# VectorE computes one head's exps in 53 of 512 attention bursts

## Chip, cores, metric

The kernel runs on one core of one Trainium2 chip. The metric is the device time of one execution in microseconds (us). Executions of one kernel agree here within about 0.3%. A trace is one profiled execution; its span is 1.7 to 1.8 us shorter than the time of the same execution. Engines: PE is TensorE (PEld its weight loads), ACT is ScalarE, DVE is VectorE.

## The reference

The result mixes a state-space layer and an attention layer by a gate, `g * a + (1 - g) * b`, over 2048 rows of 1024 columns. What matters here is the attention `b`: 32 heads of 32 columns, no mask.

```python
q, k, v = qkv[0], qkv[1], qkv[2]
scores = jnp.einsum("bhqd,bhkd->bhqk", q, k) * (Dh ** -0.5)
p = _softmax(scores, axis=-1)
o = jnp.einsum("bhqk,bhkd->bhqd", p, v)
```

The exps of 32 x 2048 x 2048 scores are most of ScalarE's work. The layer `a`, the projections and the output product are "dense" work that TensorE does between the attention's parts.

## The kernel before

The attention is cut into 512 bursts of four heads, 256 keys and 256 queries. A burst has three parts: eight score matmuls, two exps of 128x1024 (two heads each), and value sums in four quarters of four matmuls. Scores live in three PSUM slots of two banks. A burst takes two slots, so the scores of the next burst must wait until the first exp of this one has freed its slot.

```python
def burst(self, B):
    sl = [(2 * self.p) % 3, (2 * self.p + 1) % 3]
    # ... eight score matmuls into slots sl[0] and sl[1] ...
    for z in range(2):
        s, p = sl[z], self.pt_of(B, z)
        self.act(lambda e, s=s, p=p: e.activation(self.tile[p], ps[:, 2 * s:2 * s + 2, :],
                 ACT.Exp, scale=SCALE), [("S", s)], [("pt", p)], "exp")
```

Bank 6 holds the value sums. Bank 7 is the only bank of the dense work. A dense "chain" is eight matmuls of 512 columns (or sixteen, with four small diagonal ones) that accumulate in bank 7; VectorE then evicts it, and the next chain's first matmul must wait for that eviction. Each burst of the main loop is ordered so:

```python
for p in range(first, NBURST):
    self.burst(p)                       # scores, then the two exps
    q0, q1 = self.quarters[p]
    self.pv(q0, q1)                     # value sums of burst p-2, in general 4 quarters
    if q1 % 32 == 0:
        self.normalize(q1 // 32 - 1)    # VectorE
    # ... DMA issues ...
    while used < quota:                 # quota 4: four dense matmuls, in order
        # ... choose a chain where none is open ...
        wt, f = cur.pieces.pop(0)
        f()
        used += wt
        # ...
    # ... VectorE's background work, as much as fits the period ...
    if ended is not None:
        ended.evac()                    # VectorE evicts bank 7
```

## Time and profile before

| | before |
|---|---|
| time, median | 961.46 us |
| ACT busy | 944.0 of 960.1 us |
| start of one burst's first exp to the next burst's, from burst 128 on | 1.833 us |
| so one 128x1024 exp occupies ACT's pipe for | 0.917 us |
| length of that exp's record in steady state | 1.326 us |

The last two rows need care. Exp records overlap: one is 1.326 us long, yet the next starts 0.917 us later. A record therefore holds some queueing behind its predecessor.

Next, the timeline of the kernel before over one burst in which a new dense chain begins (start us, length us, engine, line, operation; in brackets the idle time before and what ended it). L1393 evicts bank 7, L1559 is the scores, L1582 the value sums, L1386 the dense matmuls.

```profile
465.86 0.69 DVE L1393 CAST f_Q<-f_ps 128x512 bf16<-128x512 f32 x1 [2.94 <-PE f_ps L1386]
465.89 0.12 PEld L1559 LDWEIGHTS f_ps<-f_Q,f_K 32*128 32x128 bf16 x8 [0.56 <-ACT f_pt L1565]
466.22 0.47 PEld L1582 LDWEIGHTS f_ps<-f_V,f_pt 128*128 128x128 bf16 x16 [0.21 <-issue]
466.61 0.55 PEld L1386 LDWEIGHTS f_ps<-f_xT,f_wb 128*128 128x128 bf16 x4
...
467.72 0.12 PEld L1559 LDWEIGHTS f_ps<-f_Q,f_K 32*128 32x128 bf16 x8 [0.56 <-ACT f_pt L1565]
```

The reader should see two things. The scores are released by ACT, so TensorE has slack at the end of the burst. And the eviction starts slightly before the scores and ends at 466.55.

### The profile page before, as it was taken

To read this page: it belongs to the slowest core of one execution; us is meant where nothing else is said; L and a number is where in the kernel's file an instruction comes from. 1 tells how busy PE (TensorE), PEld (TensorE's weight loads), DVE (VectorE), ACT (ScalarE), POOL (GpSimd) and SP (SyncE) were. 2 spreads that over 40 slices of the span, in tenths; PEclk is the share of its full clock that TensorE was granted. 3 is DMA by queue.
4 is the path that set the end of the run, shared out by engine and by line. 5 is a ranking of instruction groups with operands and counts; after the bars stand their busy time and mean duration, and the time that the engine had idled before them with its cause. 6 is when DMAs were issued, how large, how long until landed. Compare 5 with 4: busy or idle time off the path is not lost.

```text
span 960.1 us, 33364 instructions
## 1 busy us (share of the span) xinstructions
PE 928.0 (97%) x15316; PEld 490.1 (51%) x15316; DVE 513.2 (53%) x1097; ACT 944.0 (98%) x1034; POOL 10.1 (1%) x39
## 2 busy tenths in 40 slices
PE   8899999999999999999999999999999999999996
PEld 4555644564444554555545654544645556444443
DVE  2788888898888427112188711178836112232223
ACT  6999999999999999999999999999999999999996
POOL 2000000000000000000000000000000000000000
PEclk9999999999999999999999999999999999999998
DMA  9558434210133002220023210133101213123312
GB/s 203 96 103 131 77 59 85 60 28 29 49 67 79 17 8 62 58 53 17 18 52 62 59 40 24 43 85 60 40 6 39 84 38 118 51 80 118 106 59 72
DMA packets 157074, 60.88 MB, mean 63 GB/s; under 512 B 145664, under 2 KB 145664, under 8 KB 156928
## 3 DMA queue, kind: packets, MB, share of 16 engines
q1 hardware_dynamic: 154768, 58.16, 27.0%
q8 instruction: 121, 1.98, 0.9%
q10 hardware_dynamic: 2160, 0.53, 0.3%
q14 instruction: 25, 0.20, 0.1%
HBM read 16.79 MB, written 12.58 MB: 31 GB/s over the span
## 4 chain that ended last, share of the span: by engine, by line
ACT 96%; SPq 1%; PE 1%; DVE 1%; DMA 1%; issue 0%; DVEq 0%
ACT f_pt L1565 89%; ACT f_OT L1565 2%; ACT f_Et L1565 2%; ACT f_cT_re L1565 2%; ACT f_cT_im L1565 2%; SPq L1040 1%; DMA f_xT<-in_A_x_dram 1%; PE f_ps L1559 0%; PE f_ps L1789 0%; PE f_ps L1582 0%; PE f_ps L1161 0%; PE f_ps L1416 0%; DVE f_xT L1828 0%; PE f_ps L1121 0%; PE f_ps L1815 0%
## 5 line engine op out<-in xcount | busy, mean ns | idle before, releaser
L1565 ACT ACTIVATE f_pt<-f_ps 128x1024 bf16<-128x1024 f32 x944 | 867.1, 1309 | 0.6 <-PE f_ps L1559 0.6
L1582 PEld LDWEIGHTS f_ps<-f_V,f_pt 128*128 128x128 bf16 x7552 | 220.2, 96 | 99.2 <-issue 98.8
L1582 PE MATMUL f_ps<-f_V,f_pt 128*128 128x33 bf16 x7552 | 268.7, 178 | 0.0
L1559 PE MATMUL f_ps<-f_Q,f_K 32*128 32x256 bf16 x4096 | 203.3, 273 | 22.7 <-ACT f_pt L1565 4.4
L1559 PEld LDWEIGHTS f_ps<-f_Q,f_K 32*128 32x128 bf16 x4096 | 60.5, 92 | 224.2 <-ACT f_pt L1565 205.8
L1416 PE MATMUL f_ps<-f_xT,f_wb 128*128 128x512 bf16 x512 | 131.0, 377 | 0.5 <-DVE f_pf L1211 0.4
L1386 PE MATMUL f_ps<-f_xT,f_wb 128*128 128x512 bf16 x464 | 118.9, 378 | 0.0
L1335 DVE TENSOR_TENSOR_SCAN f_ht<-f_pf,f_init,f_ut 128x512 bf16<-128x512 f32 x64 | 80.8, 1273 | 0.0
L1458 DVE TENSOR_SCALAR f_Ag<-f_ps,f_gcol 128x512 f32<-128x512 f32 x32 | 24.0, 751 | 91.0 <-PE f_ps L1445 91.0
L1445 PE MATMUL f_ps<-f_cT_im,f_hp 128*128 128x512 bf16 x192 | 72.6, 378 | 0.0
L1445 PE MATMUL f_ps<-f_cT_re,f_hp 128*128 128x512 bf16 x192 | 72.6, 378 | 0.0
L1595 DVE RECIPROCAL f_rc<-f_ps 128x8 f32<-128x8 f32 x63 | 13.1, 208 | 107.3 <-PE f_ps L1582 107.1
L1476 PE MATMUL f_ps<-f_wb,f_OT 128*128 128x512 bf16 x252 | 65.8, 380 | 0.0
L1404 PE MATMUL f_ps<-f_wb,f_xT 128*128 128x128 bf16 x896 | 59.2, 219 | 0.0
L1416 PEld LDWEIGHTS f_ps<-f_xT,f_wb 128*128 128x128 bf16 x512 | 40.5, 96 | 31.9 <-issue 0.4
L1482 DVE SCALAR_TENSOR_TENSOR f_xT<-f_ps,f_gcol,f_hp 128x512 bf16<-128x512 f32 (+1 forms) x28 | 21.0, 750 | 62.5 <-PE f_ps L1476 62.5
L1422 DVE CAST f_ub<-f_ps 128x512 bf16<-128x512 f32 x48 | 33.2, 691 | 39.7 <-PE f_ps L1416 39.7
L1386 PEld LDWEIGHTS f_ps<-f_xT,f_wb 128*128 128x128 bf16 x464 | 36.3, 96 | 27.9
L1404 PEld LDWEIGHTS f_ps<-f_wb,f_xT 128*128 128x128 bf16 x896 | 50.4, 97 | 0.0
L1326 DVE TENSOR_TENSOR f_tq<-f_ht,f_Et 128x512 bf16<-128x512 bf16 x128 | 45.8, 416 | 0.0
L1393 DVE CAST f_Q<-f_ps 128x512 bf16<-128x512 f32 x30 | 20.7, 692 | 46.7 <-PE f_ps L1386 46.5
L1326 DVE TENSOR_TENSOR f_ut<-f_tq 128x512 f32<-128x512 bf16 x64 | 42.2, 683 | 0.0
(130 smaller groups left out, 619.8 us busy)
## 6 DMA issues: line engine op xcount, KB each, us to landing
ag_scratch<-f_Ag SPq DMA_DIRECT2D x32, 256.0 KB, 2.3
f_hp<-ag_scratch SPq DMA_DIRECT2D x32, 256.0 KB, 2.8
f_wb<-in_B_wqkv_dram SPq DMA_DIRECT2D x21, 256.0 KB, 4.2
out_dram<-f_xT SPq DMA_DIRECT2D x16, 256.0 KB, 2.1
f_wb<-in_B_wo_dram SPq DMA_DIRECT2D x1, 1024.0 KB, 5.5
f_OT<-f_On SPq DMA_TRANSPOSE x63, 2.3
f_wb<-in_B_wo_dram SPq DMA_DIRECT2D x1, 768.0 KB
f_wb<-in_B_wqkv_dram ACTq DMA_DIRECT2D x2, 256.0 KB, 4.0
```

The source lines that it names most:

```text
L1326: ops.append((c, lambda: dve(lambda e: e.tensor_tensor(o, a, b, op), r, w)))
L1335: ops.append((1.29, lambda ri=ri: dve(lambda e: e.tensor_tensor_scan(ht[:, ri, :], rr, ut[:, ri, :], self.init[:, ri, j:j + 1], ALU.mult, ...
L1386: mms.append((1, lambda e, f, l, a=a: e.matmul(ps[:, bank, :], w[:, g % 2, part, a, :], xT[:, a, 512 * ch:512 * (ch + 1)], start=f, stop=l ...
L1404: m = e.matmul(ps[:, bank, 128 * q:128 * (q + 1)], xT[:, a, 128 * kt:128 * (kt + 1)], w[:, g % 2, 2, a, :], start=(a == 0), stop=(a == 7))
L1416: mms.append((1, lambda e, f, l, a=a: e.matmul(ps[:, 7, :], bT[:, n % 2, ri, a, :], xT[:, a, 512 * ch:512 * (ch + 1)], start=f, stop=l), [ ...
L1422: self.dve(lambda e: e.tensor_copy(self.ub[k][:, ri, :], ps[:, 7, :]), [("bank", 7)], [("ub", k, ri)] + over, "evac_u")
L1445: mms.append((1, lambda e, f, l, j=j, ri=ri: e.matmul(ps[:, 7, :], hp[:, ri, j, cols], cT[ri][:, j, 512 * cb:512 * (cb + 1)], start=f, sto ...
L1458: self.dve(lambda e: e.tensor_scalar(a, ps[:, 7, :], self.gcol[:, 0, tt:tt + 1], None, ALU.mult), [("bank", 7), "g0"], [at], "evac_c")
L1476: mms.append((1, lambda e, f, l, j=j: e.matmul(ps[:, 7, :], OT[:, j, 256 * qb + 128 * r:256 * qb + 128 * (r + 1)], wo[j][0][:, 512 * cb:51 ...
L1559: m = e.matmul(ps[:, 2 * sl[h // 2] + h % 2, 256 * kl:256 * (kl + 1)], K[32 * h:32 * h + 32, g % 2, 128 * kt:128 * (kt + 1)], Q[32 * h:32 ...
L1565: self.act(lambda e, s=s, p=p: e.activation(self.tile[p], ps[:, 2 * s:2 * s + 2, :], ACT.Exp, scale=SCALE), [("S", s)], [("pt", p)], "exp")
L1582: m = e.matmul(ps[:, 6, o:o + 33], self.tile[p][:, h2, 256 * kl + 128 * qt:256 * kl + 128 * (qt + 1)], V[:, g % 2, 2 * i + kl, h, :], star ...
```

## The change

The intent is to relieve ScalarE. In 53 bursts (one in four, in stretches where VectorE has little else: bursts 173 to 185, 205 to 253, 297 to 329, 401 to 505) ScalarE computes only one of the first tile's two heads. VectorE computes the other: the scaled score goes to a 32-bit integer, its upper half gives the exponent bits, its lower half feeds a cubic. TensorE's work is moved to make the changed burst short (planned at 1.41 us instead of 1.83): it gets three dense matmuls and three value quarters, the burst before it five and three, and later bursts five quarters. Value sums may now lag, so a tile's last value sums are ordered ahead of the exp that refills it.

```diff
+DPERIOD = 1.41
+for lo, hi, m in ((172, 188, 4), (204, 254, 4), (296, 332, 4), (400, 508, 4)):
+    out += [B for B in range(lo, hi) if B % m == 1]          # DVB, 53 bursts
 ...
+def dve_exp(self, B, s, p):
+    # over: at the first use of each of three tile sets, the former users of that space
+    self.act(lambda e: e.activation(t[:, 0, :], ps[:, 2 * s, :], ACT.Exp, scale=SCALE), [("S", s)], [("pt", p)] + over, "exp")
+    self.dve(lambda e: e.tensor_scalar(xi, ps[:, 2 * s + 1, :], EXP_A, EXP_B, ALU.mult, ALU.add), [("S", s)], [("xi", k)] + over, "exp_a")
+    self.dx += [  # put into VectorE's order later, where they fit
+        (0.48, ... e.tensor_scalar(hi, hi, 0.0, 128.0, ALU.max, ALU.mult) ...),        # exp_b
+        (0.73, ... e.scalar_tensor_tensor(xw, lo, EXP_C2, lo, ALU.add, ALU.mult) ...), # exp_c
+        (0.73, ... e.scalar_tensor_tensor(xw, xw, EXP_C1, lo, ALU.add, ALU.mult) ...), # exp_d
+        (0.73, ... e.scalar_tensor_tensor(t[:, 1, :], xw, EXP_C0, ev, ALU.add, ALU.mult) ...)]  # exp_f
 ...
-            self.burst(p)
-            self.pv(q0, q1)
+            second = self.burst(p)          # scores and the first exp
+            self.pv(self.quarters[p])
+            second()                        # the second exp, behind the value sums
 ...
+            cap = 5                         # value quarters
+            if p in DVB or p + 1 in DVB:
+                cap = 3
 ...
-            quota = MM_PER_PERIOD if p >= FIRST + 0 else 0
+            quota = 3 if p in DVB else 5 if p + 1 in DVB and (cur is None or cur.left >= 8) else MM_PER_PERIOD
```

More of the change, by code (lines that the diff above doesn't have):

```diff
@@ L9 @@
 I32 = mybir.dt.int32
+I16 = mybir.dt.int16
+U16 = mybir.dt.uint16
 ACT = mybir.ActivationFunctionType
@@ L23 @@
 RC_MIN = 1e-10
-RC_MAX = 1e20
+RC_MAX = 1e12
 class Op:
@@ L929, with dve_bursts @@
 MM_PER_PERIOD = 4
+DPERIOD = 1.41
+EXP_A = 16713.9646930418
+EXP_B = 4936176.0
+EXP_C2 = 189883.03836007958
+EXP_C1 = 38303098318.667244
+EXP_C0 = 3607248267949745.0
+def dve_bursts():
+    out = []
+    for lo, hi, m in ((172, 188, 4), (204, 254, 4), (296, 332, 4), (400, 508, 4)):
+        out += [B for B in range(lo, hi) if B % m == 1]
+    return out
+DVB = set(dve_bursts())
 REST = 508
@@ L1004, in __init__ @@
         self.tile += [self.cT[ri][:, j, :].rearrange("p (h n) -> p h n", h=2) for j in range(8) for ri in range(2)]
+        row6 = self.OT[:, 6, :].rearrange("p (t h n) -> p t h n", t=2, h=2)
+        row7 = self.OT[:, 7, :]
+        hx = [hp[:, r, 4:8, :].rearrange("p a n -> p (a n)") for r in range(2)]
+        hx0 = hx[0].rearrange("p (t h n) -> p t h n", t=2, h=2)
+        self.xt = [hx0[:, 0], hx0[:, 1], row6[:, 0], row6[:, 1], ub[:, 0], ub[:, 1]]
+        self.xi = [hx[1][:, 0:1024].bitcast(I32), row7[:, 0:1024].bitcast(I32), self.ut[:, 0, :].bitcast(I32)]
+        self.xw = [hx[1][:, 1024:2048].bitcast(F32), row7[:, 1024:2048].bitcast(F32), self.ut[:, 1, :]]
+        self.tile += self.xt
         self.wv0 = self.OT[:, 0, 0:1040].rearrange("p (a n) -> p a n", a=8)
@@ L1176, in opening @@
             elif op == "B":
-                self.burst(8 * U + i)
+                self.burst(8 * U + i)()
                 while self.later and self.later[0][0] <= self.p:
@@ L1344, in item_ops @@
         hw = ["warm"] if ch == 0 and j == 0 else []
+        if ch == 2 and j >= 4:
+            hw = self.x_toks(0)
         if b == 1 and j == 0:
@@ L1511, in plan @@
     def plan(self):
-        self.quarters, done = {}, 0
+        self.quarters = {}
         used = {}
-        for p in range(FIRST, NBURST + 1):
-            n = min(4 * (p - 1), done + (12 if p < FIRST + 0 else 5), done // 32 * 32 + 32)
-            left = done // 32 * 32 + 32 - done
-            if 5 < left < 13 and 4 * (p - 1) >= done + 6:
-                n = done + 6
-            self.quarters[p] = (done, n)
-            for q in range(done, n):
-                used[q // 4] = p
-            done = n
+        parts = []
+        for B in range(NBURST):
+            for q in range(4):
+                late = B in DVB and q == 1
+                parts.append((B + 2 + (2 if late else 0), B, q))
+        todo = [sorted(parts[32 * U:32 * U + 32]) for U in range(NBURST // BURSTS)]
+        done = 0
+        for p in range(FIRST, NBURST + 1):
+            cap = 5
+            if p in DVB or p + 1 in DVB:
+                cap = 3
+            unit = todo[done // 32]
+            left = len(unit)
+            ready = [t for t in unit if t[0] <= p]
+            n = min(cap, len(ready))
+            if 5 < left < 13 and len(ready) >= 6 and cap == 5 and p < 200:
+                n = 6
+            if left == cap + 1 == len(ready) and p >= 100:
+                n += 1
+            self.quarters[p] = [(B, q) for _, B, q in unit[:n]]
+            for _, B, q in unit[:n]:
+                used[B] = p
+            del unit[:n]
+            done += n
+            if not unit and done % 32:
+                assert False
         order = [8 * int(w[1]) + int(w[3]) for w in self.OPENING.split() if w[0] == "B"]
@@ L1542, in plan, with x_set, x_of, x_toks @@
             self.pt_at[b] = t
+        self.ring_at, k, x = {}, 2 * RING, 0
+        for B in range(RING, NBURST):
+            for z in range(2):
+                if B in DVB and z == 0:
+                    self.ring_at[B, z] = self.x_of(B, x % 2)
+                    x += 1
+                else:
+                    self.ring_at[B, z] = k % 6
+                    k += 1
+    def x_set(self, B):
+        return 0 if B < 254 else 1 if B < 392 else 2
+    def x_of(self, B, n):
+        return len(self.tile) - 6 + 2 * self.x_set(B) + n
+    def x_toks(self, k):
+        return [(n, len(self.tile) - 6 + 2 * k + t) for n in ("pt", "ptd") for t in range(2)] + [("xi", k), ("xw", k)]
     def pt_of(self, B, z):
-        return self.pt_at[B][z] if B < RING else (2 * B + z) % 6
+        return self.pt_at[B][z] if B < RING else self.ring_at[B, z]
     def burst(self, B):
@@ L1562, in burst, with exp @@
         self.S.op("pe", mm, reads=[("K", g % 2, i // 2), ("Q", qz)], writes=[("S", sl[0]), ("S", sl[1])], name="qk")
-        for z in range(2):
-            s, p = sl[z], self.pt_of(B, z)
-            self.act(lambda e, s=s, p=p: e.activation(self.tile[p], ps[:, 2 * s:2 * s + 2, :], ACT.Exp, scale=SCALE), [("S", s)], [("pt", p)], "exp")
-    def pv(self, q0, q1):
+        self.exp(B, 0, sl[0])
+        return lambda: self.exp(B, 1, sl[1])
+    def exp(self, B, z, s):
+        ps, p = self.ps, self.pt_of(B, z)
+        assert self.left_in.get(p, 0) == 0, (B, z)
+        self.left_in[p] = 2
+        self.holds[p] = (B, z)
+        if z == 0 and B in DVB:
+            self.dve_exp(B, s, p)
+        else:
+            self.act(lambda e: e.activation(self.tile[p], ps[:, 2 * s:2 * s + 2, :], ACT.Exp, scale=SCALE), [("S", s)], [("pt", p)], "exp")
@@ new lines, in dve_exp @@
+    def dve_exp(self, B, s, p):
+        ps, k = self.ps, self.x_set(B)
+        xi, xw, t = self.xi[k], self.xw[k], self.tile[p]
+        halves = xi.bitcast(U16).rearrange("p (n two) -> p n two", two=2)
+        lo, hi = halves[:, :, 0], xi.bitcast(I16).rearrange("p (n two) -> p n two", two=2)[:, :, 1]
+        ev = xi.bitcast(BF).rearrange("p (n two) -> p n two", two=2)[:, :, 1]
+        over = []
+        if not self.seen_x[k]:
+            self.seen_x[k] = True
+            if k == 0:
+                assert self.c_left[0] == 0
+                over = [("hp", 0, j, ri) for j in range(8) for ri in range(2)]
+            elif k == 1:
+                assert self.c_left[1] == 0
+                over = [("hp", 1, j, ri) for j in range(8) for ri in range(2)]
+            else:
+                assert self.items_done == 32, (self.p, self.items_done, self.log[216:336])
+                over = [("ut", 0), ("ut", 1)] + [("ub", a, b) for a in range(2) for b in range(2)]
+        self.act(lambda e: e.activation(t[:, 0, :], ps[:, 2 * s, :], ACT.Exp, scale=SCALE), [("S", s)], [("pt", p)] + over, "exp")
+        self.dve(lambda e: e.tensor_scalar(xi, ps[:, 2 * s + 1, :], EXP_A, EXP_B, ALU.mult, ALU.add), [("S", s)], [("xi", k)] + over, "exp_a")
+        I, W = ("xi", k), ("xw", k)
+        assert not self.dx, (self.p, [c for c, _ in self.dx], self.log[-8:])
+        self.waiting.add(B)
+        self.dx += [(0.48, lambda: self.dve(lambda e: e.tensor_scalar(hi, hi, 0.0, 128.0, ALU.max, ALU.mult), [I], [I], "exp_b")),
+                    (0.73, lambda: self.dve(lambda e: e.scalar_tensor_tensor(xw, lo, EXP_C2, lo, ALU.add, ALU.mult), [I], [W], "exp_c")),
+                    (0.73, lambda: self.dve(lambda e: e.scalar_tensor_tensor(xw, xw, EXP_C1, lo, ALU.add, ALU.mult), [I, W], [W], "exp_d")),
+                    (0.73, lambda: self.dve(lambda e: e.scalar_tensor_tensor(t[:, 1, :], xw, EXP_C0, ev, ALU.add, ALU.mult), [I, W], [("ptd", p)], "exp_f")),
+                    (0.0, lambda: self.waiting.discard(B))]
@@ L1569, in pv, with mm @@
+    def pv(self, quarters):
         ps, V = self.ps, self.V
-        for q in range(q0, q1):
-            B, z, kl = q // 4, q // 2 % 2, q % 2
+        for B, q in quarters:
             U, i = divmod(B, BURSTS)
             g = U // QUNITS
+            z = q // 2
             p = self.pt_of(B, z)
-            def mm(e, z=z, p=p, kl=kl, i=i, g=g):
+            split = B in DVB and z == 0
+            todo = [(kl, q) for kl in range(2)] if split else [(q % 2, h2) for h2 in range(2)]
+            begin = i == 0 and q == 0
+            assert self.holds[p] == (B, z)
+            self.left_in[p] -= 1
+            assert not (begin and split) and not (split and q and B in self.waiting)
+            def mm(e, z=z, p=p, todo=todo, i=i, g=g, begin=begin):
@@ L1577, in mm @@
                 m = None
-                for h2 in range(2):
+                for kl, h2 in todo:
                     for qt in range(2):
@@ L1582, in mm @@
                         m = e.matmul(ps[:, 6, o:o + 33], self.tile[p][:, h2, 256 * kl + 128 * qt:256 * kl + 128 * (qt + 1)], V[:, g % 2, 2 * i + kl, h, :],
-                                     start=(i == 0 and z == 0 and kl == 0 and h2 == 0 and qt == 0), stop=(i == BURSTS - 1 and kl == 1),
+                                     start=(begin and h2 == 0 and qt == 0), stop=(i == BURSTS - 1 and kl == 1),
                                      skip_group_check=True)
                 return m
-            kw = dict(writes=["O"]) if i == 0 and z == 0 and kl == 0 else dict(acc=["O"])
-            self.S.op("pe", mm, reads=[("pt", p), ("V", g % 2, i // 2), "v1"], name="pv", **kw)
+            kw = dict(writes=["O"]) if begin else dict(acc=["O"])
+            self.S.op("pe", mm, reads=[("ptd" if split and q else "pt", p), ("V", g % 2, i // 2), "v1"], name="pv", **kw)
     def normalize(self, U):
@@ L1604, in normalize @@
                 x += [("ub", k, ri) for k in (2, 3) for ri in range(2)]
+        if qb == 0 and g >= 6:
+            assert all(self.x_set(B) != 1 or B < U * BURSTS - 8 for B in DVB)
+            x += self.x_toks(1)
         self.dma(lambda e: e.dma_start_transpose(self.OT[:, g, 256 * qb:256 * (qb + 1)].rearrange("p (t q) -> p t q", t=2),
@@ L1615, in build @@
         self.later, self.tabled, self.folded = [], [], []
+        self.holds, self.left_in = {}, {}
+        self.dx, self.seen_x, self.waiting = [], [False] * 3, set()
         self.bg2 = []
@@ L1660, in build @@
         self.c_end = 0
+        tnext = 0.0
+        nq = 0
         log = self.log = []
@@ L1665, in build @@
             self.p = p
-            self.burst(p)
-            t0 = PERIOD * (p - first)
-            period = PERIOD
-            q0, q1 = self.quarters[p]
-            self.pv(q0, q1)
-            if q1 % 32 == 0:
-                self.normalize(q1 // 32 - 1)
+            second = self.burst(p)
+            t0 = tnext
+            period = DPERIOD if p in DVB else PERIOD
+            tnext = t0 + period
+            if p in DVB:
+                self.dve_t = max(self.dve_t, t0 + 0.3) + 0.75
+            self.pv(self.quarters[p])
+            second()
+            nq += len(self.quarters[p])
+            if nq % 32 == 0 and self.quarters[p]:
+                self.normalize(nq // 32 - 1)
                 self.dve_t = max(self.dve_t, t0 + PE_HEAD) + 0.75
@@ L1703, in build @@
             used = 0.0
-            quota = MM_PER_PERIOD if p >= FIRST + 0 else 0
+            quota = 3 if p in DVB else 5 if p + 1 in DVB and (cur is None or cur.left >= 8) else MM_PER_PERIOD
+            base = quota
             ended = None
@@ L1744, in build @@
                     cur = None
-                elif used >= quota and cur.left <= 1 and quota == MM_PER_PERIOD:
+                elif used >= quota and cur.left <= 1 and quota == base:
                     quota += 1
             log.append((p, ended.tag if ended else (cur.tag if cur else None), used, round(self.dve_t - t0, 2), len(self.bg) + len(self.bg2)))
-            limit = t0 + (period - 0.1 if ended is not None else period + PE_HEAD)
-            while self.bg or self.bg2:
+            limit = t0 + (period - 0.1 if ended is not None else period + (0.1 if p + 1 in DVB else PE_HEAD))
+            while self.dx:
+                c, fn = self.dx[0]
+                st = max(self.dve_t, t0)
+                if st + c > limit:
+                    break
+                self.dx.pop(0)
+                fn()
+                self.dve_t = st + c
+            while not self.dx and (self.bg or self.bg2):
                 src = self.bg if self.bg and (self.bg[0][2] in self.tabled or not self.bg2) else self.bg2
@@ L1766, in build @@
         self.log = log
-        assert not outs and cur is None
+        assert not outs and cur is None and nq == 4 * NBURST - 8
         self.tail()
@@ L1774, in tail @@
         z = self.ut[:, 1, 0:65]
-        dve(lambda e: e.memset(z, 0.0), [], ["z"] + [("ut", 1)])
+        dve(lambda e: e.memset(z, 0.0), [], ["z"] + [("ut", r) for r in range(2)] + self.x_toks(2))
+        assert not self.dx, (self.p, [c for c, _ in self.dx], self.log[-8:])
         def check(u0, u1, s0, s1, c):
@@ L1791, in tail @@
         check(0, 63, 0, 63, 0)
-        self.pv(4 * NBURST - 8, 4 * NBURST - 4)
+        self.pv([(NBURST - 2, q) for q in range(4)])
         preload()
-        self.pv(4 * NBURST - 4, 4 * NBURST)
+        self.pv([(NBURST - 1, q) for q in range(4)])
         ov = ps[:, 6, 0:264].rearrange("p (a c) -> p a c", a=8)
```

## The prediction

> **What bounds the kernel now.** ScalarE. The engine summary has it busy 944.0 of 960.1 us (98%); the chain of waits that ended last is 96% ScalarE, 89% of it the exps, and it idles 0.6 us before the 944 exps of the largest group. From burst 128 on, the starts of the first exps of successive bursts are 1.833 us apart, so one 128x1024 exp occupies the pipe for 0.917 us. TensorE shows 97%, but its ends are modelled: its weight loads wait in nearly every burst until an exp frees a score slot (206 us in the list of waits). Its issue per burst is about 0.33 us scores, 0.41 us for 16 value sums and 0.86 us dense, 1.60 of 1.83 us. VectorE is 53% busy, and where the 53 bursts lie (about 327-356, 386-477, 556-618, 745-943 us) mostly 6 to 18 us in 40.
>
> **Removed.** In 53 bursts a 512-wide head leaves ScalarE. From the lone exps and copies of this trace (128x512 0.597 us, 128x256 0.383, 128x128 0.278) an element costs about 0.83 ns; the Trainium skill, "ScalarE: Activation LUTs", section "What ACT_TABLE_LOAD costs", states 0.833 ns and a fixed part per instruction, and 0.917 us per 1024 agrees (0.853 + 0.064). The half exp should occupy 0.49 us: 0.427 us saved each, 22.6 us in all.
>
> **Added.** VectorE gets five instructions per burst. From like ones here: 0.75 us (512-wide scalar op from PSUM, as the gate's eviction), 0.48 to 0.7 (16-bit in place, stride two), three scalar_tensor_tensor of 0.68 to 0.75: about 3.4 us, 180 us in all, so VectorE goes to about 690 us. TensorE's work is only moved (3 dense pieces and 3 value quarters in such a burst, 5 pieces before it).
>
> **On the critical path.** All of the 22.6 us, if the score slot still comes back in time. First exp's end to the scores' start is 0.056 us, scores 0.40, then 0.05 to the next exp: with an unqueued exp of 1.05 us the loop is about 1.55 of 1.83 us, so 0.28 us slack. In a changed burst VectorE's first op frees the slot last: 0.05+0.75+0.06+0.40+0.05 = 1.31 against a period of 1.41. That holds when VectorE is idle at the start: dense chains start at even bursts and changed bursts are 1 mod 4, so chains end in or after the changed burst and their evictions do not sit ahead of it. TensorE then needs about 1.29 of 1.41, and 1.72 of 1.83 in the burst before. I allow 1 to 2 us for late VectorE starts and full TensorE periods. The early value sums only let a tile be refilled in the burst that reads it last.
>
> **Predicted time:** 940.0 us, range 937.5 to 945. Faster by over 2% (below 942.4) 0.75, within 2% 0.25, slower 0.0.
>
> **What would show it.** ScalarE's busy time near 921 us, without gaps, over 95% of the chain; 53 half exps with the next exp starting about 0.49 us after; changed bursts 1.41 us long, the others 1.833; VectorE near 690 us; the scores' wait for the exps shrunk by some 10 us; few waits of scores for VectorE.
>
> **What would make it wrong.** The half exp occupying over 0.49 us; VectorE's first op starting late behind an eviction or a normalization, so that the scores, then ScalarE, wait for VectorE; 5 dense pieces with 5 value quarters overfilling TensorE's period; value sums waiting for VectorE's cubic. Each 0.1 us per changed burst costs 5 us.

## More of the kernel before

The page of the kernel before: busy time by engine, the chain that ended last, and its first group (line, engine, operation, output and input, count; then busy us and mean ns of one; then ACT's idle time ahead of it).

```profile
PE 928.0 (97%) x15316; PEld 490.1 (51%) x15316; DVE 513.2 (53%) x1097; ACT 944.0 (98%) x1034; POOL 10.1 (1%) x39
...
ACT 96%; SPq 1%; PE 1%; DVE 1%; DMA 1%; issue 0%; DVEq 0%
...
L1565 ACT ACTIVATE f_pt<-f_ps 128x1024 bf16<-128x1024 f32 x944 | 867.1, 1309 | 0.6 <-PE f_ps L1559 0.6
```

ScalarE is the limit: the chain runs through it and it hardly waits.

(Within a run of value sums, and from them to an unhindered dense chain, weight loads start 0.025 us apart; what goes beyond that I count as wait.) In the stretches of bursts that are changed later, 56 new chains wait already in this kernel, 0.03 to 0.12 us each, 4.2 us in all. It costs nothing, because TensorE then waits for ACT anyway.

## The result, and the profile after

The time fell from 961.46 to 951.12 us. The ratio is 0.9894, 95% interval 0.988 to 0.9908: within 2%, and outside the predicted range of 937.5 to 945. (A ratio here is the mean time of one kernel's fast runs over the mean of the other's from the same rounds, so it is not quite the ratio of the medians quoted.) Half of the expected gain is missing.

The page after, with the lines that answer to those above; L1639 is the exp of 1024 columns, L1660 the half exp.

```profile
PE 890.4 (94%) x15095; PEld 491.4 (52%) x15316; DVE 677.5 (71%) x1362; ACT 928.6 (98%) x1034; POOL 10.1 (1%) x39
...
ACT 56%; PE 34%; DVE 5%; issue 2%; SPq 1%; DMA 1%; DVEq 0%
...
L1639 ACT ACTIVATE f_pt<-f_ps 128x1024 bf16<-128x1024 f32 x891 | 828.9, 1175 | 1.6 <-PE f_ps L1623 1.5
```

ScalarE still reads 98% busy with almost no idle time. That hides what happened: the chain is now only 56% ScalarE and 34% TensorE, and the mean exp record shrank from 1309 to 1175 ns. The work per exp did not shrink; the queueing inside the record did. In the last long stretch this is complete. Here are all full exps between 850 and 930 us, before and then after (count, then minimum, median and maximum of the length in ns):

```profile
L1565 ACT ACTIVATE f_pt<-f_ps x88: 1325/1326/1328, 849.5 to 929.3; 128x1024 bf16<-128x1024 f32 x88
```

```profile
L1639 ACT ACTIVATE f_pt<-f_ps x79: 1018/1032/1047, 849.9 to 929.7; 128x1024 bf16<-128x1024 f32 x79
```

A record of 1.02 to 1.05 us is what an exp looks like when it finds the pipe empty. So I measure lost time differently: from the end of one exp to the end of the next, less the 0.917 us (or 0.490 us for a half exp) that it occupies. I call this the empty time of the pipe. From burst 128 on it sums to 0.0 us before and 12.25 us after. The books close: 961.46 - 53 x 0.427 + 12.25 = 951.1 us. (From burst 128 on they must, by the way the empty time is defined; that they close for the whole time says that nothing was lost earlier.) The half exp did its part, since the next exp starts 0.492 us after it on average, 0.494 at most.

Where the empty time arises, as mean distance between first exps of successive bursts:

| from | before | after | ScalarE alone would need |
|---|---|---|---|
| the burst before a changed one | 1.829 | 1.998 | 1.833 |
| a changed burst | 1.833 | 1.453 | 1.407 |
| the next | 1.841 | 1.872 | 1.833 |
| the one after | 1.830 | 1.835 | 1.833 |
| four bursts | 7.333 | 7.158 | 6.907 |

The largest part is lost in the burst *before* the changed one. This is the timeline of such a burst after the change (248; burst 249, changed, begins at 465.03). L1422 evicts bank 7, L1623 is the scores, L1692 the value sums, L1415 the dense matmuls, L1661 VectorE's first op on the scores.

```profile
462.99 0.12 PEld L1623 LDWEIGHTS f_ps<-f_Q,f_K 32*128 32x128 bf16 x8 [0.42 <-ACT f_pt L1639]
...
463.10 0.69 DVE L1422 CAST f_Q<-f_ps 128x512 bf16<-128x512 f32 x1 [0.39 <-PE f_ps L1415]
463.32 0.37 PEld L1692 LDWEIGHTS f_ps<-f_V,f_pt 128*128 128x128 bf16 x12 [0.21 <-issue]
...
463.84 0.76 PEld L1415 LDWEIGHTS f_ps<-f_xT,f_wb 128*128 128x128 bf16 x5 [0.15 <-DVE f_Q L1422]
...
465.03 0.12 PEld L1623 LDWEIGHTS f_ps<-f_Q,f_K 32*128 32x128 bf16 x8 [0.42 <-issue]
...
465.48 0.69 DVE L1661 TENSOR_SCALAR f_hp<-f_ps 128x512 int32<-128x512 f32 x1 [1.69 <-PE f_ps L1623]
...
466.42 0.12 PEld L1623 LDWEIGHTS f_ps<-f_Q,f_K 32*128 32x128 bf16 x8 [0.42 <-DVE f_hp L1661]
```

In the burst ahead, 20 value sums ahead of the dense matmuls leave TensorE hardly any slack. The eviction of its chain starts 0.11 us after the scores, where it started 0.02 us before them, and ends at 463.79. The 12 value sums of burst 248 cover less of it: their last weight load starts at 463.59, and without a wait the dense one would follow 0.025 us later. TensorE stands until the eviction is done, loads at 463.84, a wait of 0.23 us (the bracket counts from the end of the last load's record), and needs 1.2 us more for five matmuls and the next scores' start. The burst takes 2.04 us where ScalarE needs 1.83. The next scores (465.03) are no longer released by ACT.

One bracket misleads: at 466.42 the page names VectorE's op on the scores as the releaser, but that op ended at 466.17. TensorE's own three matmuls came last. The experiments below check this.

(The trace after lacks some 220 matmul records; weight loads are complete, so I read TensorE from those.)

### The profile page after: what moved, and what is told of

It reads as the page before. It is cut to its first block, busy times and chain, and to the rows that moved or that the text cites. A ratio compares the mean times of both kernels' runs of the same rounds, so it can differ in the third digit from the quotient of the medians.

```text
span 949.5 us, 33488 instructions
## 1 busy us (share of the span) xinstructions
PE 890.4 (94%) x15095; PEld 491.4 (52%) x15316; DVE 677.5 (71%) x1362; ACT 928.6 (98%) x1034; POOL 10.1 (1%) x39
## 4 chain that ended last, share of the span: by engine, by line
ACT 56%; PE 34%; DVE 5%; issue 2%; SPq 1%; DMA 1%; DVEq 0%
ACT f_pt L1639 49%; PE f_ps L1692 9%; PE f_ps L1474 8%; PE f_ps L1623 6%; PE f_ps L1505 5%; PE f_ps L1415 3%; PE f_ps L1433 2%; ACT f_OT L1639 2%; ACT f_Et L1639 2%; ACT f_cT_re L1639 2%; ACT f_cT_im L1639 2%; PE f_ps L1445 1%; DVE f_xT L1511 1%; SPq L1067 1%; DMA f_xT<-in_A_x_dram 1%
## 5 line engine op out<-in xcount | busy, mean ns | idle before, releaser
L1639 ACT ACTIVATE f_pt<-f_ps 128x1024 bf16<-128x1024 f32 x891 | 828.9, 1175 | 1.6 <-PE f_ps L1623 1.5
L1692 PE MATMUL f_ps<-f_V,f_pt 128*128 128x33 bf16 x7128 | 258.4, 178 | 0.6 <-DVE f_On L1706 0.4
L1692 PEld LDWEIGHTS f_ps<-f_V,f_pt 128*128 128x128 bf16 x7128 | 210.5, 96 | 89.3 <-issue 83.0
L1623 PE MATMUL f_ps<-f_Q,f_K 32*128 32x256 bf16 x4096 | 203.3, 273 | 15.7 <-ACT f_pt L1639 2.2
L1623 PEld LDWEIGHTS f_ps<-f_Q,f_K 32*128 32x128 bf16 x4096 | 60.7, 92 | 206.2 <-ACT f_pt L1639 147.2
L1445 PE MATMUL f_ps<-f_xT,f_wb 128*128 128x512 bf16 x448 | 117.2, 377 | 10.1 <-issue 2.5
L1415 PE MATMUL f_ps<-f_xT,f_wb 128*128 128x512 bf16 x406 | 106.3, 378 | 7.0 <-DVE f_Q L1422 1.4
L1505 PE MATMUL f_ps<-f_wb,f_OT 128*128 128x512 bf16 x218 | 57.7, 378 | 8.1 <-DVE f_xT L1511 4.0
L1474 PE MATMUL f_ps<-f_cT_re,f_hp 128*128 128x512 bf16 x146 | 55.1, 378 | 0.0
L1661 DVE TENSOR_SCALAR f_ut<-f_ps 128x512 int32<-128x512 f32 x27 | 18.7, 691 | 48.8 <-PE f_ps L1623 42.6
L1415 PEld LDWEIGHTS f_ps<-f_xT,f_wb 128*128 128x128 bf16 x464 | 36.2, 96 | 29.5 <-DVE f_Q L1422 0.8
L1353 DVE TENSOR_TENSOR f_tq<-f_ub,f_Et 128x512 bf16<-128x512 bf16 x96 | 34.6, 417 | 0.1
L1661 DVE TENSOR_SCALAR f_hp<-f_ps 128x512 int32<-128x512 f32 x17 | 11.7, 691 | 31.2 <-PE f_ps L1623 28.7
```

The costliest lines, as they stand in the source:

```text
L1353: ops.append((c, lambda: dve(lambda e: e.tensor_tensor(o, a, b, op), r, w)))
L1415: mms.append((1, lambda e, f, l, a=a: e.matmul(ps[:, bank, :], w[:, g % 2, part, a, :], xT[:, a, 512 * ch:512 * (ch + 1)], start=f, stop=l ...
L1445: mms.append((1, lambda e, f, l, a=a: e.matmul(ps[:, 7, :], bT[:, n % 2, ri, a, :], xT[:, a, 512 * ch:512 * (ch + 1)], start=f, stop=l), [ ...
L1474: mms.append((1, lambda e, f, l, j=j, ri=ri: e.matmul(ps[:, 7, :], hp[:, ri, j, cols], cT[ri][:, j, 512 * cb:512 * (cb + 1)], start=f, sto ...
L1505: mms.append((1, lambda e, f, l, j=j: e.matmul(ps[:, 7, :], OT[:, j, 256 * qb + 128 * r:256 * qb + 128 * (r + 1)], wo[j][0][:, 512 * cb:51 ...
L1623: m = e.matmul(ps[:, 2 * sl[h // 2] + h % 2, 256 * kl:256 * (kl + 1)], K[32 * h:32 * h + 32, g % 2, 128 * kt:128 * (kt + 1)], Q[32 * h:32 ...
```

## The experiments

Theory 1: TensorE has become the limit in these stretches, through its own work and through the new chain's wait for the eviction of bank 7. Theory 2: VectorE is late, so that it holds the score slots (through its first op) and the evictions (through the cubic). A third effect was seen in the trace before any run: at the first use of each of three tile sets, VectorE's first op waits for ScalarE's half exp.

### VectorE does nothing for the exps (e1)

```diff
-        self.dve(... exp_a ...)
-        self.dx += [exp_b, exp_c, exp_d, exp_f, done]
+        if over:   # first use of a set: fill its two half tiles with 1.0
+            for n in both_tiles: self.dve(lambda e: e.memset(self.tile[n][:, 1, :], 1.0), [], [("ptd", n)] + over, "fill")
+        self.dx += [nop, nop, nop, nop, done]
```

> The kernel after, but VectorE does none of its five instructions per changed burst (no first op on the scores, no cubic; the half tile keeps a filled constant, so the result is wrong on purpose). Theory 1 (TensorE has become the limit: its bursts with 20 value sums or five dense pieces, and the first piece of a dense chain waiting for the eviction of the chain before, take 7.03 to 7.15 us per four bursts where ScalarE needs 6.91): almost nothing changes there; only the three first changed bursts of a tile set (0.6 to 0.7 us each, a wait of VectorE for ScalarE) and two evictions behind the cubic (bursts 456 and 460, about 1 us together) come back, so 947 to 949 us. Theory 2 (VectorE's lateness holds the score slots and the evictions): near the ideal, 939 to 942 us.

Measured: 950.98 us, ratio 0.9889, empty time 12.61 us. Taking 162 us of work from VectorE (677.5 to 515.9 us) changes nothing, so theory 2 falls as the main cause. My number for theory 1 was missed by 2 us, for a reason in the experiment: the two fills of each set carry the same claim on the space, wait for ScalarE as well, and then run 0.485 us each ahead of an eviction. The empty time around the first two changed bursts of each set is 0.9 to 1.0 us per set here, against 0.5 to 0.6 before the edit, so the first use of the sets got worse instead of better. What the run did show is bursts 457 and 461: they lose 0.52 and 0.66 us after the change, and 0.0 and 0.04 us here. There the cubic did stand ahead of the eviction. (The result also passed the comparison with the reference, though I had called it wrong on purpose: constants for one head in 53 of 512 bursts stay within the tolerance. So passing it says nothing about how exact VectorE's exps are.)

### Less dense work for TensorE (e2)

```diff
-                f()
+                if not (near and wt and cur.tag != "vproj" and cur.left % 8 == 4 - (cur.n == 7)):
+                    f()      # one matmul of eight is left out in the changed stretches
```

> The kernel after, with one of eight matmuls of every dense chain left out (not of the value projections) in the stretches of the changed bursts, result wrong on purpose; nothing of ScalarE's or VectorE's work changes. It takes 0.215 us of TensorE's per chain. Theory 1: four bursts drop from 7.05 to about 6.65 us of TensorE work, under ScalarE's 6.91, so ScalarE is the limit again: 941 to 944 us. Theory 2 (VectorE late): no change beyond 1 us, 950 to 951 us.

Measured: 941.76 us, ratio 0.9788, result wrong as intended; empty time 2.45 us. VectorE and ScalarE do exactly what they did, and 9.8 of the 12.25 us return. TensorE's side is the limit. The run cannot say whether its own work or the wait for the eviction counts, as it relieves both.

### The wait at the first use of a set (e3)

```diff
+        dx = [the former writers and readers of `over`]
         self.act(... half exp ..., [("pt", p)] + over, "exp")
-        self.dve(... exp_a ..., [("S", s)], [("xi", k)] + over, "exp_a")
+        self.S.op("dve", ... exp_a ..., reads=[("S", s)], writes=[("xi", k)], deps=dx, name="exp_a")
```

> The kernel after, without the false wait at the first use of each of the three sets of tiles: there VectorE's first op is ordered behind ScalarE's half exp because both claim the space; now both wait only for the space's earlier users. Everyone who reads the trace so expects the three bursts (173, 297, 401) to fall from 2.0 to 2.1 us to about 1.4: 1.9 to 2.1 us less, 949.1 us. If the TensorE limit absorbs it, less.

Measured: 949.52 us, ratio 0.9871; 1.6 us less than the kernel after, where 2.0 was expected. Empty time 10.84, so 1.4 us of it was this wait. VectorE's first op of burst 297, in the kernel after and then here:

```profile
553.40 0.69 DVE L1661 TENSOR_SCALAR f_OT<-f_ps 128x512 int32<-128x512 f32 x1 [6.22 <-ACT f_OT L1660]
```

```profile
551.64 0.69 DVE L1662 TENSOR_SCALAR f_OT<-f_ps 128x512 int32<-128x512 f32 x1 [5.32 <-PE f_ps L1623]
```

After the change it was released by ACT's half exp (which started at 552.51 and ran for 0.86 us); here by the scores. The burst falls from 2.10 to 1.46 us. Both ops claimed the space of former users with a write, and two writes order each other, though they go to different places.

### TensorE's work not moved (e4)

```diff
-            if p in DVB or p + 1 in DVB:
-                cap = 3
-            quota = 3 if p in DVB else 5 if p + 1 in DVB and (cur is None or cur.left >= 8) else MM_PER_PERIOD
+            quota = MM_PER_PERIOD
```

> The kernel after, with TensorE's work not moved: four dense pieces and up to five value quarters in every burst, also in the changed ones. Theory 1 as a sum (TensorE's total with evictions is the limit, whatever burst it lies in): 949 to 953 us, the changed burst grows to about 1.7 us and the one before shrinks to about 1.83. Theory 1b (the moves themselves overfill the burst before and cost the gain): 943 to 946 us. Theory 2: as after, 951 us.

Measured: 953.5 us, ratio 0.9914, empty time 14.88 us. A changed burst takes 1.669 us and the one before 1.824. The move itself is right and worth 2.4 us; it is not what costs the gain. Four even bursts take 7.21 us with the waits, so spreading the work evenly does not fit it under 6.907 either. The value lies just above the range that I gave.

The trace also says that the waits for evictions do not come from the move alone. With 16 value sums, as in the kernel before, burst 248 of this run:

```profile
463.49 0.12 PEld L1621 LDWEIGHTS f_ps<-f_Q,f_K 32*128 32x128 bf16 x8 [0.42 <-ACT f_pt L1637]
463.60 0.69 DVE L1422 CAST f_Q<-f_ps 128x512 bf16<-128x512 f32 x1 [0.19 <-PE f_ps L1415]
463.82 0.47 PEld L1690 LDWEIGHTS f_ps<-f_V,f_pt 128*128 128x128 bf16 x16 [0.21 <-issue]
...
464.35 0.55 PEld L1415 LDWEIGHTS f_ps<-f_xT,f_wb 128*128 128x128 bf16 x4
```

The eviction starts 0.11 us after the scores, and the dense load comes 0.53 us after the first value sum's, where it came 0.39 us after before the change. New chains wait 14.5 us for evictions in the changed stretches here, and 12.8 us in the kernel after.

### The chain's end ahead of the value sums (e5)

This puts the disputed wait out of the way without adding or removing work. In a burst in which a chain ends, its last dense matmuls go ahead of those value sums that no refill waits for. The eviction then runs beside value sums.

```diff
+            first_dense = near and cur is not None and cur.left <= quota and (nq + len(self.quarters[p])) % 32 != 0
+            now, rest = self.quarters[p], []
+            if first_dense:      # now: up to the last quarter that reads the tile refilled in this burst
+                n = max([i + 1 for i, (B, q) in enumerate(now) if self.pt_of(B, q // 2) == self.pt_of(p, 1)] or [0])
+                now, rest = now[:n], now[n:]
-            self.pv(self.quarters[p])
+            self.pv(now)
             second()
             # ... dense matmuls as before ...
+            if first_dense:
+                self.pv(rest)
```

It contains e3's edit.

> e3_set_wait, and in the 86 bursts of the changed stretches in which a dense chain ends, the chain's last pieces stand ahead of those value sums that the next refill does not need, so that the eviction of the one dense bank runs beside value sums and the next chain's first piece need not wait for it. No work is added or removed on any engine. Theory 1 with the eviction wait as the cause: four bursts fall from 7.05-7.20 to about 6.91-6.95 us with chains of eight, from 7.09 to about 7.03 with chains of sixteen and their diagonal pieces (0.06 us a burst of TensorE's own work): 943 to 945.5 us. Rival (TensorE's own work fills the bursts, the wait is only slack): 948.5 to 950 us.

Measured: 940.65 us, ratio 0.9782 (0.9765 to 0.9798), correct: 8.9 us less than e3, and 2.4 us below the range that I gave for theory 1. Empty time fell from 10.84 to 1.74 us. This is the fastest correct version. The same place as above, bursts 247 and 248 (L1416 is the dense matmuls, L1423 the eviction, L1694 the value sums, L1624 the scores):

```profile
458.44 0.55 PEld L1416 LDWEIGHTS f_ps<-f_xT,f_wb 128*128 128x128 bf16 x4
...
459.11 0.46 PEld L1694 LDWEIGHTS f_ps<-f_V,f_pt 128*128 128x128 bf16 x8
...
459.51 0.17 PEld L1694 LDWEIGHTS f_ps<-f_V,f_hp 128*128 128x128 bf16 x4
459.53 0.69 DVE L1423 CAST f_Q<-f_ps 128x512 bf16<-128x512 f32 x1 [0.26 <-PE f_ps L1416]
...
459.71 0.12 PEld L1624 LDWEIGHTS f_ps<-f_Q,f_K 32*128 32x128 bf16 x8
...
460.04 0.37 PEld L1694 LDWEIGHTS f_ps<-f_V,f_pt 128*128 128x128 bf16 x12 [0.21 <-issue]
...
460.34 0.77 PEld L1416 LDWEIGHTS f_ps<-f_xT,f_wb 128*128 128x128 bf16 x5
...
461.53 0.12 PEld L1624 LDWEIGHTS f_ps<-f_Q,f_K 32*128 32x128 bf16 x8 [0.42 <-ACT f_pt L1640]
```

The four last matmuls of the chain stand ahead of twelve value sums. The eviction starts 0.18 us before the next scores instead of 0.11 us after them, and the new chain's weights load right behind the value sums, with no bracket. Burst 248 takes 1.82 us instead of 2.04, and ACT is the releaser again. The page of this kernel, chain by engine, and its exps between 850 and 930 us:

```profile
ACT 94%; SPq 2%; DVE 1%; PE 1%; DMA 1%; issue 0%; DVEq 0%
```

```profile
L1640 ACT ACTIVATE f_pt<-f_ps x82: 1139/1264/1330, 849.6 to 928.5; 128x1024 bf16<-128x1024 f32 x82
```

The records hold queueing again (median 1264 ns), so ScalarE is the limit again.

The weight loads show the wait itself: in the changed stretches new chains wait 13.3 us for evictions in e3 and 1.5 us here. A rival would be that the new order shortens TensorE's own sequence, since scores now follow value sums in 86 bursts. It is small: 20 value sums and four dense matmuls without a wait take 1.800 us in e3 and 1.792 to 1.796 us in the new order, 12 and three take 1.385 and 1.376 us at best. At 0.01 us in 86 bursts, it explains 0.9 of the 9.1 us at most (an estimate from these lengths).

### Half as many changed bursts (e6)

```diff
-    for lo, hi, m in ((172, 188, 4), (204, 254, 4), (296, 332, 4), (400, 508, 4)):
+    for lo, hi, m in ((172, 188, 8), (204, 254, 8), (296, 332, 8), (400, 508, 8)):
```

With e3's edit, 27 changed bursts.

> e3_set_wait with every second changed burst only: 27 instead of 53, one in eight. Theory 1: ScalarE saves 27 x 0.427 = 11.5 us, and TensorE, at about 14.1 us per eight bursts with the waits, stays just under ScalarE's 14.24, so nearly all of it is realized: 950 to 951.5 us, within 2 us of the kernel with all 53. Rival (each changed burst loses a fixed share of its 0.427 us, about half): 955 to 956 us.

Measured: 954.49 us, ratio 0.9924, between the two expectations: 0.5 us below the rival's, and 3 us above theory 1's. ScalarE saves 11.5 us and the pipe is empty for 4.03 us, 0.15 per changed burst, against 10.84 / 53 = 0.20 in e3. Theory 1 as a plain sum over eight bursts was too simple. The trace shows why: between two changed bursts late in the last stretch (473 and 481) the exp records stay at 1.02 to 1.05 us. Seven unchanged bursts in between do not let ScalarE's queue build up again, because without the reordering TensorE and the evictions need as long as ScalarE there too (1.845 us a burst from 474 to 479). Then each burst with the five dense matmuls is lost anew.

### No diagonal matmuls (e7), and the reordering alone (e8)

```diff
 # e7: e5, and
-        for q in range(4):
+        for q in range(0):     # the four 128-column diagonal matmuls of a chain of sixteen
 # e8: the kernel before, and
+            first_dense = near and cur is not None and cur.left <= MM_PER_PERIOD and q1 % 32 != 0
+            if not first_dense:
                 self.pv(q0, q1)
             # ... dense matmuls ...
+            if first_dense:
+                self.pv(q0, q1)
```

> e5_dense_first without the four diagonal matmuls (128 columns each) in every chain of sixteen; result wrong on purpose. In e5_dense_first ScalarE's pipe still stands empty for 1.7 us in all, 1.2 us of it in the stretches with chains of sixteen, where four bursts take 7.01 us and not 6.91. Theory 1 says that this rest is TensorE's own work there: 1.2 us less, 939.4 us, and four bursts at 6.91 there. If it is something else (VectorE beside it): no change, 940.6 us.

Measured: 938.99 us, ratio 0.9765, wrong as intended. Empty time 0.67 us, all of it at bursts 457 and 461; four bursts in the stretches with chains of sixteen take 6.91 to 6.92 us. So the 1.07 us between 1.74 and 0.67 was TensorE's own work in those stretches, not a wait.

> The kernel before, with the same reordering as e5_dense_first in the same stretches and nothing else of the change. ScalarE's pipe is never empty there, so an earlier eviction cannot pay: 961.5 us, the same within 0.5 us. A reordering that is good by itself would give 956 us or less here.

Measured: 961.0 us, ratio 0.9996 (0.9982 to 1.0009). The same reordering is worth nothing in the kernel before. It pays only where ScalarE has become faster than TensorE with its waits.

## Why the prediction was wrong, point by point

- **What bounds the kernel (ScalarE):** right. The kernel before never lets the pipe run empty from burst 128 on.
- **What is removed (0.427 us per changed burst, 22.6 us):** right. The half exp occupied 0.492 us, and the books close to 0.1 us with the predicted 0.427 us. The Trainium skill, "ScalarE: Activation LUTs", section "What ACT_TABLE_LOAD costs", states 0.833 ns per element; the trace's 0.917 and 0.492 us for 1024 and 512 columns differ by 0.425 us, which is 0.830 ns per element.
- **What VectorE gets (3.4 us per burst, about 690 us in all):** right. Measured 0.69 + 0.45 + 3 x 0.69 = 3.21 us, 677.5 us in all. The 16-bit op with stride two took 0.45 us where the others took 0.69. The Trainium skill, "VectorE: DVE Perf Modes", section "Mode 2×_2P — use both read ports for one tensor", says that an op with one source tensor in SBUF may be read through both ports and that a two-tensor op may not; the two lengths agree with that, though no run separates this cause from others.
- **The score slot's loop (0.28 us slack; 1.31 of 1.41 us with VectorE's first op):** right in normal bursts, and e1 shows that VectorE's first op does not hold anything. It missed three places where that op waits for ScalarE through a shared claim (1.4 us, e3).
- **"TensorE then needs about 1.29 of 1.41, and 1.72 of 1.83 in the burst before":** this is the step that failed. Measured 1.39 in the changed burst (1.44 with chains of sixteen), 1.80 to 1.82 us in bursts with 20 value sums and four matmuls of a chain of eight, and mostly 2.04 or 2.10 in the burst before where a chain of eight begins (1.82 there in e5, without the wait). Two terms were left out. The first is about 0.1 us between the last dense matmul and the next scores: within a chain matmuls start 0.215 us apart, but from 300 us on the scores never started less than 0.310 us after a last matmul of 512 columns (e3's trace, which has all matmul records). In the kernel before this sat unseen in the slack ahead of the ACT release. The Trainium skill, "TensorEngine Tiling (Array Packing)", section "Key Properties", says that changing the tiling mode drains the engine; the scores are tiles of 32 rows and the dense matmuls of 128, so a drain would fit. In e5's trace the extra time stands ahead of the scores only: dense matmuls to value sums, both of 128 rows, keep the 0.215 us, while scores come 0.109 us after the last value sum, where value sums follow each other in 0.025. No run separates a drain from other causes that lie with the scores. The second and larger is the wait of a new chain for the eviction of bank 7. I asked only whether evictions would stand ahead of VectorE's first op, not whether the value sums would still cover them. Before, TensorE waited for ACT, the eviction mostly began 0.02 us ahead of the scores to 0.04 us after them, and what 16 value sums left uncovered was hidden in that slack. With the slack gone it begins 0.11 us after them, and a new chain waits mostly 0.03 or 0.09 us behind 20 value sums and 0.23 or 0.29 us behind the 12 of the burst before (the larger where the eviction takes 0.75 us and not 0.69). I had named a full TensorE period as a risk, but for five dense matmuls with five value quarters; the bursts that overflowed most have five with three.
- **"I allow 1 to 2 us for late VectorE starts and full TensorE periods":** measured 12.25 us. By the experiments: 9.1 us eviction waits of new chains (e5 against e3; up to 0.9 us of it may be the order itself), 1.4 us first use of the sets (e3), 1.1 us TensorE's own work with diagonal matmuls (e7), 0.7 us cubic ahead of the eviction at bursts 457 and 461 (what e7 leaves, and e1 takes away).
- **"ScalarE's busy time near 921 us, without gaps, over 95% of the chain":** wrong for the kernel after (928.6 us, 56%), close for the repaired one (922.9 us, 94%). The 940 us that I predicted is what the change gives once TensorE's order is repaired and e3's wait is gone: 940.65 us. Neither was part of the change.

Left open: the early ordering of value sums ahead of a refill was not tested alone. In 205 bursts of the changed kernel a refill needs it, so it cannot be undone without also changing how far the value sums may lag.

## What to carry to other kernels

When the limiting engine is relieved, list for the next engine not its mean busy share but its period with every wait that the old limit was hiding: here 0.1 us ahead of the scores, and the eviction of a single bank, for which new chains waited 4.2 us before the change at no cost. Before moving work between periods, check which transfer or eviction the moved work had been covering. And where records of an engine overlap, follow their lengths: a busy share that stayed at 98% while the mean record shrank from 1309 to 1175 ns meant here that the engine's queue had run dry.

## What the Trainium skill lacked or had wrong

- "Perfetto Trace Analysis", section "Identifying the Most-Contended Engine", takes occupancy as a fair measure for ScalarE. As a distance from the limit that was so here (12.25 us of empty pipe are 1.3% of the span), but it does not say whether ScalarE still sets the time: it read 98% before and after, while ScalarE's share of the chain fell from 96% to 56%. Its section on the DVE and Act engine instruction has the record begin when execution in the ALUs begins. Yet back-to-back 128x1024 exps had records of 1.326 us starting 0.917 us apart, and 1.02 to 1.05 us where they found the pipe empty: about 0.3 us of queueing lies inside the record.
- "ScalarE: Activation LUTs", section "What ACT_TABLE_LOAD costs", gives 186 ns fixed with an overlap of about 93 ns back to back, so by its figures 0.946 us per 1024 columns (an estimate from that page). The trace had 0.917 and, for 512 columns, 0.492 us: about 65 ns fixed. The page does not say for which source memory its figures hold; the exps here read PSUM. A lone exp's record, 1.02 to 1.05 us, fits its 186 ns.
- "ScalarE: Activation LUTs", section "Rules for kernel authors", calls ScalarE the only option for `exp`. VectorE computed it here by exponent bits and a cubic, at 3.21 us for 128x512 against the 0.427 us that ScalarE saves. The result passed the comparison, but so did e1 with constants in its place, so the accuracy is not shown.
- "TensorEngine Tiling (Array Packing)" gives no size for the drain at a change of tiling mode. About 0.1 us more than the spacing within a chain was seen here between 128-row matmuls and 32-row scores.
